# Attention with a 32-token window and a gated convolution FFN: the first batch's first half by head pairs, V's odd-row copies shared out anew, the order planned anew

## The chip, the cores and the metric

The kernel runs on one core of one Trainium2 chip. Its five queues are PE (TensorE, matrix products; PEld is its weight loads), DVE (VectorE), ACT (ScalarE), POOL (GpSimd) and SP, which here issues nearly all DMAs. The metric is the device time of one execution in microseconds (us), the median of several runs; lower is better.

## What is computed

The reference, cut to what matters (batch 8, 8 heads, 576 tokens, head width 64; model width 512, hidden width 1,024):

```python
scores = matmul(q, k.transpose(0, 1, 3, 2)) / sqrt(64)
scores = where(abs(pos[:, None] - pos[None, :]) <= 32, scores, -1e9)
attn = softmax(scores)
x = matmul(attn, v)             # back to (batch, tokens, 8 * 64)
h = maximum(x @ w_in, 0)
conv = conv_w[0] * h[t-1] + conv_w[1] * h[t] + conv_w[2] * h[t+1]
out = (h * sigmoid(conv)) @ w_out
```

Inputs and output are float32; the kernel computes its products in bfloat16.

## The kernel before

Everything is written out by hand. One long table, ORDER, lists some 845 steps as short words, and each step issues a few instructions at once; the order of the words is the order in which every engine's queue is filled. A word has a name, its arguments, where there is a choice a letter for the engine or the form (a is ScalarE, d VectorE, p GpSimd), and after @ the PSUM bank in which its result goes. Each engine works its queue in order, and an instruction waits where its inputs, its buffer or its bank are not free. All engine calls go through one helper, so nearly all instructions carry its line, L163, in the profile; they are told apart by the names of their tiles.

The steps, by batch b, group of four heads G (0, 1), token half h (0: the first four tiles of 64 tokens, 1: the other five):

- lq, lk load Q or K of (b, G) into one of six buffers st; cq, ck cast it to bfloat16 (qb); tq, tk turn it on VectorE in blocks of 32 (qT, kT). In batch 0 casts and turns go by halves of the columns.
- lv loads one of five chunks of V (128 tokens) into vst; cv casts it into ve. An odd tile of 64 tokens needs V at an offset of 64, so a second copy vo holds four such chunks for each batch: vo makes one chunk with two instructions (from ve, or on GpSimd from vst), and vd makes two chunks by two DMAs from ve. Such a chunk is called a pair of copies below. ve and vo carry a column of ones, which gives the softmax's sums.
- sc writes the band mask and the scores of four heads into four banks; ex is the exponential on ScalarE, into attn; av multiplies with V; nr (a reciprocal and a product on VectorE) normalises into xn.
- xp and xe (PE and ScalarE) or xt (a transposing DMA) turn xn into xT.
- ph is a projection with two of eight blocks of w_in, re its ReLU into hT. The tokens are cut in pieces of 384 columns, the first four of half that. li, ci and lo, co load and cast the quarters of w_in and w_out; block pair m needs quarter m.
- pc, tp, th, ga compute the convolution, its tanh (the sigmoid as a scaled tanh) and the gate into gT, in one of several forms: P, p on PE with full arrays; D, a, A on PE with quarter arrays, where a and A need three tanh instructions; X, x on ScalarE and VectorE; G, g on GpSimd.
- py is the output projection of 128 tokens, ye its copy into y, st its store.
- dg builds the diagonal matrices of the convolution weights, three instructions on ScalarE or one on VectorE; cw and cc bring those weights into place. id and ia are products without use, of 512 columns, that keep PE at work; ia reads a cast buffer and so waits for it. s0 to s6 are memsets and masks.

Of the kernel before, what the change touches and what calls it, by code (L numbers as in the profile page):

```python
# [17 lines left out]
s1 s3 lq,0,0 cq,0,0,1,a tq,0,0,1 cw@5 id,5@7 ia,0,0,1,1@7 lq,0,1 s4 cc lk,0,0 lv,0,2 lk,0,1 lv,0,1 cq,0,0,0,a  # L18
ia,0,0,0,3@7 lv,0,0 cq,0,1,0,p ia,0,1,0,3@7 s5 tq,0,1,0 dg,2,a ck,0,0,0,p tq,0,0,0 dg,3,d s2 dg,1,a tk,0,0,0
cq,0,1,1,a ia,0,1,1,5@7 ia,1,0,0,4@7 ck,0,0,1,a tk,0,0,1 s0 lv,0,3 dg,0,a dg,6,d sc,0,0,0@0 ck,0,1,0,p tq,0,1,1 dg,7,d  # L20
sc,0,0,1@4 ex,0,0,0 id,1@3 ia,1,1,0,2@3 lv,0,4 ck,0,1,1,p ia,1,1,1,2@3 tk,0,1,0 cv,0,2,p ex,0,0,1 li,0 li,3 tk,0,1,1
sc,0,1,0@0 cv,0,1,a cv,0,0,p sc,0,1,1@4 li,1 ex,0,1,0 vo,0,1,d vo,0,0,d av,0,1,0@0 av,0,0,0@2 nr,0,0,0 nr,0,1,0 lq,1,0
lk,1,0 ex,0,1,1 id,5@7 cv,0,3,p lk,1,1 vo,0,2,p lq,1,1 cv,0,4,a lv,1,1 dg,4,a vo,0,3,p ci,0,a lv,1,2 xp,0,1@0 xp,0,0@2
xe,0,1,a av,0,1,1@6 xe,0,0,a av,0,0,1@0 nr,0,1,1 ci,3,a ph,0,0@4 nr,0,0,1 re,0,0 ph,0,3@3 pc,0,0,P@4 re,0,3 xp,0,2@5
ci,1,p pc,0,3,p@2 cq,1,0,p xp,0,3@1 xp,0,4@6 xe,0,2,a ph,0,1@3 xe,0,3,a tq,1,0 xe,0,4,a ph,1,0@0 th,0,0,P ck,1,0,p
lv,1,0 re,0,1 ph,1,3@7 re,1,0 th,0,3,p ph,2,3@5 tk,1,0 re,1,3 ph,1,1@6 ck,1,1,p re,2,3 ga,0,0,P dg,5,d sc,1,0,0@0
re,1,1 pc,0,1,P@4 ex,1,0,0 pc,1,1,P@6 cq,1,1,p li,2 tk,1,1 sc,1,0,1@0 th,1,1,P lv,1,3 th,0,1,P pc,1,3,p@5 cv,1,1,p
# [51 lines left out]
tp,13,1,X ye,8,2,a pc,13,3,X@0 py,10,2@7 st,8,2 re,13,2 tp,13,0,g tp,13,3,X th,13,1,X pc,13,2,a@5 py,10,0@4 ye,10,2,d  # L79
th,13,3,X ga,13,1,X th,13,0,g py,9,2@7 th,13,2,a ga,13,0,g ga,13,3,X py,10,1@3 ye,10,0,a ga,13,2,a ye,9,2,a st,10,0  # L80
st,9,2 py,11,1@5 ye,10,1,d st,10,1 st,10,2 py,11,0@4 ye,11,1,a st,11,1 py,11,2,0@0 ye,11,0,a st,11,0 ye,11,2,0,a
st,11,2,0 py,11,2,1@4 ye,11,2,1,a st,11,2,1
"""


@with_exitstack
def kernel(
# [155 lines left out]
    where = {}  # L243
# [478 lines left out]
```

## Time and profile before

| what | value |
|---|---|
| median of 3 timed runs | 213.53 us (212.47 to 214.25) |
| the profiled execution | 210.9 us, span 209.1 us |
| DMA | 46.67 MB in 65,431 packets, mean 223 GB/s |
| of these under 512 B (V, mostly) | 53,084 packets |

Busy shares are read by stages: the first 20 us hold the loads, casts and scores of batch 0, from there to about 48 us the first batches' projections run while batch 1 is prepared, and from 48 us on each batch's attention stands between the projections of earlier ones. In timeline rows the first number is the start, the second the duration, and the bracket at the end the engine's idle time just before with what ended it.

### The profile page before, as it was taken

Reading aid. Unit: us, or ns where it says so; the run is one execution under the profiler, and the core shown is the slowest. Engines: PE = TensorE matmul, PEld = TensorE weight load, DVE = VectorE, ACT = ScalarE, POOL = GpSimd, SP = SyncE. Lnnn points to the kernel's source line nnn. Section 1 sums busy time; section 2 is a strip of 40 time slices with the busy share of each in tenths; the row PEclk is TensorE's granted clock in tenths of the full one; section 3 lists DMA queues with packets and bytes.
Section 4 is the critical chain, followed back from the end, with each engine's and each line's share of the span. In section 5 each row is a group of like instructions: output and inputs, shape, how many; then the busy total and the mean of one; then the engine's idle time right before and its main releaser. Section 6 shows DMA issues by size and latency. Waiting matters only on the chain.

```text
span 209.1 us, 7615 instructions
## 1 busy us (share of the span) xinstructions
PE 195.4 (93%) x3223; PEld 115.8 (55%) x3223; DVE 167.9 (80%) x277; ACT 172.0 (82%) x272; POOL 138.2 (66%) x161
## 2 busy tenths in 40 slices
PE   4978998799999989999999899998999999999994
PEld 2346986694565555655564454554655565555442
DVE  1785694989958988989999968979998749989850
ACT  3879888599889977998977878979989689999842
POOL 1485663596893859559999689889365009999600
PEclk9999999999999999999999999999999999999999
DMA  6999989989969889699998999996995541141154
GB/s 225 335 219 358 370 210 300 384 184 327 337 169 275 208 272 294 145 267 202 346 243 198 243 293 198 306 305 135 259 297 155 78 113 50 31 140 55 50 201 150
DMA packets 65431, 46.67 MB, mean 223 GB/s; under 512 B 53084, under 2 KB 55412, under 8 KB 65396
## 3 DMA queue, kind: packets, MB, share of 16 engines
q1 hardware_dynamic: 65360, 46.16, 82.6%
q8 instruction: 25, 0.41, 0.9%
q14 instruction: 10, 0.08, 0.1%
q10 hardware_dynamic: 36, 0.01, 0.0%
HBM read 32.52 MB, written 9.44 MB: 201 GB/s over the span
## 4 chain that ended last, share of the span: by engine, by line
PE 47%; DMA 12%; DVE 12%; SPq 11%; ACT 7%; issue 6%; POOL 4%; ACTq 0%; POOLq 0%
PE PS L163 47%; SPq L163 11%; DMA st<-in_k_dram 8%; DVE gT L163 5%; POOL zg L163 2%; DMA xT<-xn 2%; DMA vst<-in_v_dram 2%; DVE kT L163 2%; DVE vo L163 2%; ACT attn L163 1%; ACT z L163 1%; DVE xn L163 1%; ACT y L163 1%; POOL tap L163 1%; ACT hT L163 1%
## 5 line engine op out<-in xcount | busy, mean ns | idle before, releaser
L163 PE MATMUL PS<-xT,w_in_sb 128*128 128x385 bf16 (+3 forms) x448 | 69.2, 305 | 1.0 <-DMA xT<-xn 0.8
L163 PE MATMUL PS<-w_out_sb,gT 128*128 128x512 bf16 (+1 forms) x296 | 66.9, 374 | 0.2 <-DVE gT L163 0.2
L163 PEld LDWEIGHTS <-w_in_sb 128*128 128x128 bf16 x448 | 40.4, 98 | 23.8 <-issue 3.5
L163 ACT ACTIVATE hT<-PS 128x770 bf16<-128x770 f32 (+3 forms) x56 | 40.0, 724 | 9.0 <-PE PS L163 7.2
L163 ACT ACTIVATE attn<-PS 128x1024 bf16<-128x1024 f32 (+1 forms) x32 | 36.0, 1131 | 10.5 <-PE PS L163 10.5
L163 PEld LDWEIGHTS <-gT 128*128 128x128 bf16 x296 | 27.7, 98 | 30.4 <-issue 1.4
L163 POOL TENSOR_SCALAR qb<-st 128x1152 bf16<-128x1152 f32 (+1 forms) x24 | 28.1, 1179 | 21.2 <-DMA st<-in_k_dram 11.9
L163 POOL TENSOR_TENSOR zg<-zg,tap 128x768 f32<-128x768 f32 x18 | 33.3, 1848 | 1.5
L163 ACT ACTIVATE z<-PS 64x384 f32<-64x384 f32 (+4 forms) x55 | 28.2, 514 | 1.0 <-PE PS L163 0.2
L163 DVE TENSOR_TENSOR xn<-PS,rec 128x512 bf16<-128x512 f32 (+1 forms) x32 | 26.4, 824 | 1.1
L163 DVE SCALAR_TENSOR_TENSOR PS<-hT,conv_w_sb,PS 128x384 f32<-128x384 bf16 (+1 forms) x40 | 21.4, 597 | 6.3 <-ACT PS L163 6.1
L163 DVE SCALAR_TENSOR_TENSOR gT<-z,hT 128x768 bf16<-128x768 f32 (+1 forms) x28 | 25.7, 928 | 0.8 <-ACT z L163 0.7
L163 DVE SCALAR_TENSOR_TENSOR gT<-PS,hT 128x384 bf16<-128x384 f32 (+2 forms) x38 | 23.1, 613 | 2.8 <-ACT PS L163 2.4
L163 DVE STREAM_TRANSPOSE qT<-qb 128x576 uint32<-128x576 uint32 (+1 forms) x18 | 20.1, 1128 | 6.3 <-ACT qb L163 3.7
L163 PE MATMUL PS<-hT,diag_w 64*64 64x384 bf16 (+3 forms) x354 | 23.4, 306 | 0.6 <-DVE xn L163 0.6
L163 POOL TENSOR_SCALAR zg<-hT,conv_w_sb 128x384 f32<-128x384 bf16 x18 | 12.6, 712 | 16.9 <-ACT hT L163 16.7
L163 POOL TENSOR_SCALAR tap<-hT,conv_w_sb 128x384 f32<-128x384 bf16 x36 | 23.3, 660 | 0.6
L163 POOL TENSOR_SCALAR ve<-vst 128x512 bf16<-128x512 f32 x25 | 16.8, 683 | 10.2 <-DMA vst<-in_v_dram 10.1
L163 DVE STREAM_TRANSPOSE kT<-qb 128x576 uint32<-128x576 uint32 (+1 forms) x18 | 20.1, 1129 | 1.6 <-POOL qb L163 1.5
L163 ACT COPY y<-PS 128x512 f32<-128x512 f32 (+1 forms) x25 | 14.0, 570 | 5.0 <-PE PS L163 4.8
L163 POOL TENSOR_SCALAR vo<-vst 64x512 bf16<-64x512 f32 x24 | 15.6, 649 | 1.9 <-DMA vst<-in_v_dram 0.2
L163 PEld LDWEIGHTS <-diag_w 64*64 64x64 bf16 (+1 forms) x354 | 13.8, 103 | 5.3 <-issue 2.9
(50 smaller groups left out, 219.3 us busy)
## 6 DMA issues: line engine op xcount, KB each, us to landing
st<-in_q_dram SPq DMA_DIRECT2D x16, 576.0 KB, 6.6
st<-in_k_dram SPq DMA_DIRECT2D x16, 576.0 KB, 6.8
out_dram<-y SPq DMA_DIRECT2D x35, 256.0 KB, 3.7
vst<-in_v_dram SPq DMA_DIRECT2D x24, 256.0 KB, 5.3
vst<-in_v_dram SPq DMA_DIRECT2D x16, 192.0 KB, 5.9
xT<-in_moe_w_in_dram SPq DMA_DIRECT2D x2, 512.0 KB, 5.8
xT<-in_moe_w_out_dram SPq DMA_DIRECT2D x2, 512.0 KB, 9.4
vo<-ve SPq DMA_DIRECT2D x6, 130.0 KB, 3.0
```

The lines of the kernel that those rows point to most:

```text
L163: return lambda *args, **kwargs: tc.keep_in_program_order(do(*args, **kwargs))
```

## The change

ex, av and nr take an optional head pair: they then handle two of the four heads, and av needs one bank, not two. Only the first half of batch 0 uses it. The code:

```diff
-    def ex(b, G, h):
+    def heads(pair):
+
+        return (2 * pair[0], 2) if pair else (0, 4)
+
+    def ex(b, G, h, *pair):
         bank = where["sc", b, G, h]
         attn, n = attn_of(b, G, h)
+        a0, na = heads(pair)
         scalar.activation(
-            attn.rearrange("p (a x) -> p a x", a=4), PS[:, bank:bank + 4, 0:n],
+            attn.rearrange("p (a x) -> p a x", a=4)[:, a0:a0 + na, :],
+            PS[:, bank + a0:bank + a0 + na, 0:n],
             AF.Exp, bias=0.0, scale=scale,
         )
...
-    def nr(b, G, h):
-        bank = where["av", b, G, h]
+    def nr(b, G, h, *pair):
+        bank = where[("av", b, G, h, *pair)]
         n = (len(tiles_of(h)) + 1) // 2
...
+        a0, na = heads(pair)
...
-        rec = rec_[(2 * unit(b, G) + h) % 3][:, :, 0:n]
+        rec = rec_[(2 * unit(b, G) + h) % 3][:, a0:a0 + na, 0:n]
```

The rest is the table, which is new from end to end. A line of it before and now:

```diff
-s1 s3 lq,0,0 cq,0,0,1,a tq,0,0,1 cw@5 id,5@7 ia,0,0,1,1@7 lq,0,1 s4 cc lk,0,0 lv,0,2 lk,0,1 lv,0,1 cq,0,0,0,a
+s1 lq,0,0 s0 lk,0,0 lq,0,1 lk,0,1 lv,0,1 lv,0,2 s2 cw@0 id,4@7 cc dg,7,a cq,0,0,0,p ia,0,0,0,1@7 dg,5,a cq,0,0,1,p
```

Counted over the table:

| step | before | now |
|---|---|---|
| odd-row pairs on ScalarE, VectorE, GpSimd, by DMA | 0, 14, 12, 6 | 8, 10, 6, 8 |
| casts of Q and K on ScalarE: whole, half | 8, 4 | 5, 2 |
| the same on GpSimd | 20, 4 | 23, 6 |
| V chunks on ScalarE, GpSimd | 15, 25 | 14, 26 |
| weight quarters of w_in on ScalarE, GpSimd | 2, 2 | 1, 3 |
| diagonals on ScalarE, VectorE | 4, 4 | 5, 3 |
| outputs on ScalarE, VectorE | 25, 12 | 27, 10 |
| taps in forms P and p; D, a and A; X and x; G and g | 15; 22; 10; 9 | 12; 26; 9; 9 |
| products without use | 31 | 19 |

ScalarE's eight pairs lie in batches 0 (chunks 2, 3), 3 (2, 3), 4 (0, 1) and 5 (0, 1). Three places show how instructions moved. The first is GpSimd at the start, from its first work on the inputs. st0 holds Q and st1 K of batch 0's first heads, st2 and st3 those of its other heads; vst0 is V as loaded, xT1 and hT2 hold weight quarters. Before:

```order
L163 TENSOR_SCALAR qb2_69<-st2_63 128x576
L163 TENSOR_SCALAR qb1_68<-st1_62 128x576
L163 AFFINE_SELECT band0_115<-band0_115 128x256 x2
L163 MEMSET vst0_77 32x512 x2
L163 TENSOR_SCALAR qb3_70<-st3_64 128x576 x2
L163 TENSOR_SCALAR ve0_78<-vst0_77 128x8x64 x3
L163 TENSOR_SCALAR vo0_80<-vst0_77 64x8x64 x4
L163 TENSOR_SCALAR w_in_sb0_110<-xT1_92 128x4x256
```

The same place now:

```order
L163 MEMSET vst0_77 32x512 x2
L163 AFFINE_SELECT band0_115<-band0_115 128x256 x2
L163 TENSOR_SCALAR qb0_67<-st0_61 128x576 x2
L163 TENSOR_SCALAR qb1_68<-st1_62 128x576
L163 TENSOR_SCALAR qb2_69<-st2_63 128x576
L163 TENSOR_SCALAR qb3_70<-st3_64 128x576 x2
L163 TENSOR_SCALAR ve0_78<-vst0_77 128x8x64 x4
L163 TENSOR_SCALAR w_in_sb0_110<-xT1_92 128x4x256
L163 TENSOR_SCALAR w_in_sb0_110<-hT2_95 128x4x256
```

Memsets and mask moved ahead of all casts, the first Q came here from ScalarE, the four odd-row copies went to ScalarE, and a second weight quarter came in.

The second place is VectorE around the normalisation of batch 1 (vo1, ve1 and xn1 are batch 1's). Before:

```order
L163 COPY vo1_81<-ve1_79 64x520 x4
L163 SCALAR_TENSOR_TENSOR gT0_96<-z0_103,hT0_93 128x2x192
L163 RECIPROCAL rec1_87<-PS_118 128x4x2
L163 TENSOR_TENSOR xn1_90<-PS_118,rec1_87 128x4x2x64
L163 RECIPROCAL rec0_86<-PS_118 128x4x2
L163 TENSOR_TENSOR xn1_90<-PS_118,rec0_86 128x4x2x64
L163 COPY vo1_81<-ve1_79 64x520 x4
L163 SCALAR_TENSOR_TENSOR gT0_96<-z1_104,hT0_93 128x2x192
```

And now:

```order
L163 COPY vo1_81<-ve1_79 64x520 x4
L163 SCALAR_TENSOR_TENSOR gT1_97<-z2_105,hT1_94 128x2x192
L163 RECIPROCAL rec0_86<-PS_118 128x4x2
L163 TENSOR_TENSOR xn1_90<-PS_118,rec0_86 128x4x2x64
L163 RECIPROCAL rec1_87<-PS_118 128x4x2
L163 TENSOR_TENSOR xn1_90<-PS_118,rec1_87 128x4x2x64
L163 SCALAR_TENSOR_TENSOR gT1_97<-PS_118,hT1_94 128x2x192
```

The second group of four copies has left VectorE; GpSimd has it, reading vst.

The third place is SP's queue where batch 3 is loaded (st0 to st5 are the buffers of Q and K; st3 is here K of batch 3's second heads; out is a store). Before:

```order
L163 DMA st2_63<-in_q_dram 128x1152
L163 DMA vst0_77<-in_v_dram 128x8x64
L163 DMA out_0_dram<-y0_99 128x512
L163 DMA st5_66<-in_k_dram 128x1152
L163 DMA out_0_dram<-y1_100 128x512
L163 DMA vst0_77<-in_v_dram 128x8x64
L163 DMA vst0_77<-in_v_dram 96x8x64
```

And now:

```order
L163 DMA vst0_77<-in_v_dram 128x8x64
L163 DMA st2_63<-in_q_dram 128x1152
L163 DMA st3_64<-in_k_dram 128x1152
L163 DMA out_0_dram<-y2_101 128x512
L163 DMA out_0_dram<-y1_100 128x512
L163 DMA vst0_77<-in_v_dram 128x8x64
L163 DMA out_0_dram<-y0_99 128x512
```

K's load into st3 stands ahead of the first stores; before it was issued behind both stores and two loads of V. Earlier in the same queue, the third weight quarter of w_in was behind the first three V chunks of batch 1 and is now ahead of them.

More of the change, by code (lines that the diff above doesn't have):

```diff
@@ L23 @@
[L23 to L27, printed above, removed]
@@ L289, in av @@
         ts = tiles_of(h)
-        for a in range(4):
+        for a in range(a0, a0 + na):
             for i in range((len(ts) + 1) // 2):
```

139 lines of the change are left out of this document (73 added, 66 removed).

## Prediction

> **What bounds the kernel now.** I read the page's head first, then the busy time by stretches, then the timeline of the first 45 us, and last the waits of single rows. The profiled execution took 210.9 us, 209.1 of them its span.
>
> ```profile
> span 209.1 us, 7615 instructions
> PE 195.4 (93%) x3223; PEld 115.8 (55%) x3223; DVE 167.9 (80%) x277; ACT 172.0 (82%) x272; POOL 138.2 (66%) x161
> ```
>
> The stretches (span of time, its length, then busy time of PE, PEld, DVE, ACT, POOL, the granted clock, the DMA share, GB/s):
>
> ```profile
> 0.00:30.00 30.00, 24.54 (x491) 17.11 (x491) 19.17 (x50) 23.65 (x43) 17.02 (x29) 1.00 0.96 285
> 30.00:60.00 30.00, 27.34 (x543) 20.19 (x542) 24.71 (x45) 24.96 (x47) 19.81 (x24) 1.00 0.95 289
> 45.00:139.00 94.00, 92.12 (x1587) 51.72 (x1585) 83.81 (x124) 80.17 (x119) 74.08 (x82) 1.00 1.03 255
> 139.00:161.00 22.00, 21.07 (x399) 11.71 (x398) 19.97 (x31) 20.61 (x31) 15.91 (x20) 1.00 0.81 211
> 161.00:200.00 39.00, 38.93 (x429) 20.62 (x428) 32.34 (x52) 34.12 (x54) 23.46 (x24) 1.00 0.29 77
> ```
>
> From 45 us on TensorE (PE) is the bound: it is busy 152.1 of 155 us up to 200. Of the first 60 it lacks 8.1, and part of what it does there are idle products that fill waits. So a new order can win at the start, and only a little later. The table keeps nearly all of PE's work: the same projections, scores and outputs, and 12 idle products fewer. The convolution taps change form (in half-width pieces 3 fewer on full arrays, 4 more on quarter arrays), which I price below. So what counts is where PE waits.
>
> **The start.** These rows carry batch 0 up to its first projection (start, duration, engine, what; in brackets the idle time before and what ended it):
>
> ```profile
> 3.10 0.59 PE L163 MATMUL PS<-ident,conv_w 24*128 24x24 f32 x2 [3.10 <-DMA conv_w<-in_moe_conv_w_dram]
> 6.07 0.67 POOL L163 TENSOR_SCALAR qb<-st 128x576 bf16<-128x576 f32 x1 [4.75 <-DMA st<-in_q_dram]
> 6.27 1.86 ACT L163 ACTIVATE diag_w<-ident,conv_w_sb 128x128 bf16<-128x128 bf16 x6 [0.55 <-DVE hT L163]
> 8.46 0.67 POOL L163 TENSOR_SCALAR qb<-st 128x576 bf16<-128x576 f32 x1 [1.72 <-DMA st<-in_k_dram]
> 9.16 1.26 DVE L163 STREAM_TRANSPOSE kT<-qb 128x288 uint32<-128x288 uint32 x2 [0.75 <-POOL qb L163]
> 10.90 0.41 PE L163 MATMUL PS<-qT,kT 32*128 32x64 bf16 x32
> 14.08 1.53 DVE L163 COPY vo<-ve 64x520 bf16<-64x520 bf16 x4 [0.36 <-ACT ve L163]
> 15.34 0.22 PE L163 MATMUL PS<-ve,attn 128*64 128x65 bf16 x1 [0.71 <-ACT attn L163]
> 18.27 0.61 PE L163 MATMUL PS<-ident,xn 128*128 128x128 bf16 x8 [0.56 <-DVE xn L163]
> 19.83 1.36 PE L163 MATMUL PS<-xT,w_in_sb 128*128 128x193 bf16 x11
> 20.48 1.04 POOL L163 TENSOR_SCALAR w_in_sb<-xT 128x1024 bf16<-128x1024 f32 x1 [2.23 <-DMA xT<-in_moe_w_in_dram]
> ```
>
> Before, K's first load is the third in the queue and its cast starts at 8.46. In the new order it is second; second place ended in time for a cast at 6.07. The second half of K is now cast by ScalarE behind nine of its diagonal products (six take 1.86, so nine 2.8). They can start once the convolution weights have come through PE (3.69) and been copied, near 4.0, so that cast runs about 6.9 to 7.6, the two turns to about 8.9, and the first scores stand near 9.1 instead of 10.9: 1.8 earlier. The odd-row copies still wait for V's chunks, which the same bytes precede as before, and for ScalarE, which has six more diagonal products and a half cast (2.6), the first exponentials (2.4 by the rows below) and a cast of V (0.6) to do from 7.6 on: it ends near 13.1, four copies of 1.53 near 14.6, and the first product with V stands at 14.7 instead of 15.3.
>
> Then comes the split by head pairs, whose cost is in these rows (busy us, mean ns of one):
>
> ```profile
> L163 ACT ACTIVATE attn<-PS 128x1280 bf16<-128x1280 f32 x16 | 19.8, 1240 | 3.6 <-PE PS L163 3.5
> L163 DVE TENSOR_TENSOR xn<-PS,rec 128x768 bf16<-128x768 f32 x16 | 15.3, 957 | 0.6
> L163 ACT ACTIVATE attn<-PS 128x1024 bf16<-128x1024 f32 x16 | 16.3, 1022 | 6.9 <-PE PS L163 6.9
> L163 DVE TENSOR_TENSOR xn<-PS,rec 128x512 bf16<-128x512 f32 x16 | 11.1, 691 | 0.6
> L163 DVE RECIPROCAL rec<-PS 128x8 f32<-128x8 f32 x16 | 3.2, 199 | 4.9 <-ACT ve L163 2.6 <-PE PS L163 1.4 <-ACT attn L163 0.8
> ```
>
> 256 more columns cost an exponential 218 ns and a normalising product 266 ns. By that line half an exponential of 1,024 takes 0.59, so two take 0.15 more than one; half a product takes 0.42, and with a second reciprocal of 0.20 two halves cost 0.36 more than one whole. VectorE's four halves end about 2.5 after the first can start, and they start about 1.5 earlier than the two wholes did. I put the first projection at about 19.0 instead of 19.83. But this does not pass through. The second quarter of the input weights is now cast by ScalarE, and the load that it waits for let the same cast start at 20.48 before. The bytes ahead of it are the same, so it runs 20.5 to 21.5, and ScalarE's first three ReLUs, all projections with that quarter and the tap products stand behind it. So I take **0** for the start, with 0.9 gained (the load lands earlier) and 1.0 lost (the ReLUs queue) as bounds.
>
> **Batch 1, 33 to 42 us.** Here PE waits four times in the old order, beside V's late chunks:
>
> ```profile
> 34.10 0.22 PE L163 MATMUL PS<-ve,attn 128*64 128x65 bf16 x1 [0.48 <-issue]
> 34.78 0.62 POOL L163 TENSOR_SCALAR ve<-vst 128x512 bf16<-128x512 f32 x1 [1.54 <-DMA vst<-in_v_dram]
> 34.93 0.21 DVE L163 RECIPROCAL rec<-PS 128x8 f32<-128x8 f32 x1 [2.59 <-ACT ve L163]
> 36.74 2.10 DVE L163 COPY vo<-ve 64x520 bf16<-64x520 bf16 x4
> 36.76 0.51 PE L163 MATMUL PS<-ident,xn 128*128 128x128 bf16 x6 [0.54 <-DVE xn L163]
> 38.88 0.19 PE L163 MATMUL PS<-vo,attn 128*64 128x65 bf16 x1 [0.43 <-DVE vo L163]
> 41.89 0.66 PE L163 MATMUL PS<-hT,diag_w 128*128 128x192 bf16 x6 [0.64 <-DVE xn L163]
> 37.87 0.44 PE L163 MATMUL PS<-hT,diag_w 64*64 64x192 bf16 x12
> ```
>
> VectorE does one thing after another: it idles 2.59, normalises, copies two odd-row pairs for 2.10 while the next products with V wait for them, and only then normalises again. The waits of PE in these rows, 0.48, 0.54, 0.43 and 0.64, sum to 2.1. The new order loads weight quarter 2 ahead of V of batch 1, puts the two late odd-row pairs on GpSimd, which idles there (1.54 before a cast of V), and runs two more projections and, net, two more tap steps on PE ahead of the first product with V. Walking the new order with these durations, the first product with V comes when its exponential frees the banks, with the normalisation directly behind it, and 2.10 has gone from VectorE's queue. I take **2.0** gained; bounds are 2.9, when the gaps under the waits' threshold go too, and 0, when the weight quarter lands late and the third projections wait for it instead.
>
> The taps: three full-array steps of 0.66 fewer and four quarter-array steps of 0.44 more are -0.2, and the scattered quarter form has three tanh instead of one. I take 0.
>
> **Batch 3's K load.** The old order holds it behind two stores, which wait for their results:
>
> ```profile
> 62.34 1.62 SPq L163 DMA_DIRECT2D st<-in_k_dram  x1
> 68.97 3.73 POOL L163 TENSOR_SCALAR qb<-st 128x1152 bf16<-128x1152 f32 x2 [4.25 <-DMA st<-in_k_dram]
> 73.98 0.42 PE L163 MATMUL PS<-qT,kT 32*128 32x64 bf16 x32 [0.60 <-DVE kT L163]
> ```
>
> GpSimd waits 4.25 for it and PE at last 0.60. The new order issues it ahead of both stores. **0.6** gained, bounds 0 and 0.6: past 0.6 PE had other work.
>
> **The odd-row copies.**
>
> ```profile
> L163 DVE COPY vo<-ve x28: 290/292/1887, 14.1 to 114.4; 64x520 bf16<-64x520 bf16 x28
> L163 ACT CAST ve<-vst 128x512 bf16<-128x512 f32 x15 | 9.3, 624 | 0.0
> L163 ACT CAST qb<-st 128x1152 bf16<-128x1152 f32 x8 | 9.3, 1159 | 1.4 <-DMA st<-in_k_dram 1.3
> ```
>
> VectorE's copies take 0.29 at least and up to 1.89. The trace shows none on ScalarE: the rows nearest are a cast of 512 columns, 0.62, and the small diagonal product, 0.31. I take 0.55, as the width is the cast's. Sixteen are 8.8 us (5.0 to 10). ScalarE gives up three whole casts of Q and K (3.5), two halves, one weight cast and one V cast, and takes some diagonal products, outputs and tanh, so its work grows by about 5. In 45 to 139 it idles 94 - 80.2 = 13.8, which can hide that. I take **0.3** lost, bounds 0 and 5. VectorE has eight copies fewer (2.3 us at least) and two outputs fewer; it wasn't the bound, so 0. The fourth pair moved by DMA adds two transfers of 130 KB; I take 0, at worst 1.
>
> The Trainium skill's page "SBUF — State Buffer" (SBUF: two separate sides) says that VectorE in a fast mode and GpSimd take turns at a shared port, each holding it for a whole instruction, and that ScalarE never waits there. The spread from 0.29 to 1.89 in the row above agrees; by that rule the move to ScalarE costs less than its 16 durations suggest, as copies that can be stretched leave VectorE and GpSimd.
>
> **The sum.** 0 - 2.0 - 0.6 + 0.3 = -2.3: a span of 206.8. The profiled run lies 2.6 below the median of the three timed runs, 213.53 (212.47 to 214.25), so I put the change on the median: **211.2**. Around 1%, here 2.1 us, is what a measurement can tell from no change.
>
> **Rivals.**
> *The loads take it back (same).* The DMA share is 1.03 from 45 to 139: if the engines' queues are full, an earlier PE only meets the same landings, and the 2.0 of batch 1 returns as waits like the 4.25 at 68.97. For it: the share. Against it: PE is busy 92.1 of 94 there, and the old order's stores, not the engines, held the K load back. Time: 213.2 (212.4 to 214).
> *ScalarE's queue (slower).* The eight pairs stand in a first-in queue ahead of exponentials and ReLUs in batches 0, 3, 4 and 5. For it: in 139 to 161 ScalarE is busy 20.6 of 22, so it has stretches without slack. Against it: the 13.8 of slack between 45 and 139, where these pairs lie. It decides once more than 2.6 of the 5 us reach PE (the 2.3 of the sum and the 0.3 in it); with all 5 it gives 211.2 + 4.7 = 215.9.
> *PE at half rate.* The weight loads ahead of the idle products show its pace:
>
> ```profile
> 8.29 0.15 PEld L163 LDWEIGHTS <-ident 128*128 128x128 bf16 x1 [0.28 <-issue]
> 8.75 1.60 PEld L163 LDWEIGHTS <-ident 128*128 128x128 bf16 x8 [0.30 <-issue]
> 16.47 1.24 PE L163 MATMUL PS<-ident 128*128 128x512 bf16 x5
> ```
>
> Up to 8.3 one product takes 0.43, from 8.75 on 0.20, although the granted clock reads 1.00. Before the first scores the new order has 9 products where 21 stood, with holes between them. If PE still runs at half rate until the projections, the first scores (0.4), the products with V and the transposes (0.6) and the first two projections (1.4, as eleven products took 1.36) take twice as long: 2.4 lost, 211.2 + 2.4 = 213.6. For it, the holes; against it, PE kept its pace through the holes between 11 and 16 us, as five products near 17 take 1.24. The Trainium skill's page "TensorE: Matmul & The Clock Gate" (Part 1: The HAM clock gate) says that PE starts at half clock and is released by about 3.4 us of sustained activity; by that rule nine products with holes may not release it. The trace agrees with the release, at 8.3 or so.
>
> **How the numbers follow.** Forecast 0.56: its own range is 208.2 (0.9 + 2.9 + 0.6 gained, less the noise of a median) to 212.8 (1.0 lost at the start and 0.6 of batch 1's gain); 0.46 of it lies below 211.4, 0.10 above. Loads take it back: 0.21, all same. ScalarE's queue: 0.17, slower. Half rate: 0.06, of it 0.02 same and 0.04 slower with the ReLUs queued too. Faster 0.46, same 0.33, slower 0.21. The range runs from 208.2 to 215.8, up to ScalarE's rival; what it leaves out is that rival's upper part and a start that gains more than its bounds.
>
> **What would show it.** Right: first scores near 9.1 but the first tap products still near 22; no wait of VectorE of over 1 us between 32 and 42, and PE's step in batch 2 some 2 us earlier; no wait of GpSimd for K near 69. Wrong: ScalarE busy over 92% in 75 to 115 with PE waiting for its exponentials (second rival); GpSimd still waiting some 4 us for K near 69 (first); products of 0.43 after 10 us (third). The forecast fails outright if PE's new waits after 45 us, anywhere, sum to more than 2.

## The result, and the profile after

The changed kernel takes 218.44 us in the median of four runs (216.51 to 221.57), the old one on the same chip 213.0 (212.08 to 214.25): ratio 1.029, 95% interval 1.020 to 1.037. It is 5.4 us slower; 211.2 was forecast. Ratios here leave out executions over 1.5% above the fastest of their kernel. The profiled execution took 216.5 us; the head of its page, and the same stretches as before (span, length, busy PE, PEld, DVE, ACT, POOL, granted clock, DMA share, GB/s):

```profile
span 214.7 us, 7620 instructions
PE 193.0 (90%) x3217; PEld 115.5 (54%) x3241; DVE 165.7 (77%) x268; ACT 178.1 (83%) x290; POOL 133.9 (62%) x156
...
45.00:139.00 94.00, 87.81 (x1497) 48.84 (x1509) 75.12 (x109) 81.73 (x122) 66.30 (x75) 1.00 0.97 239
139.00:161.00 22.00, 21.19 (x398) 12.04 (x403) 19.21 (x29) 19.47 (x31) 13.93 (x16) 1.00 0.97 228
161.00:200.00 39.00, 35.94 (x464) 20.01 (x468) 31.55 (x48) 31.29 (x47) 21.23 (x23) 1.00 0.39 92
```

From 45 to 139 us TensorE was busy 92.1 and is now 87.8, and in the last stretch 38.9 and now 35.9. From 45 to 139 every engine but ScalarE does less, and ScalarE is busy 81.7 of 94: no engine became the bound. The start, in the timeline:

```profile
8.93 0.29 PE L163 MATMUL PS<-ident,band 32*128 32x128 bf16 x8
13.50 0.40 PE L163 MATMUL PS<-ident,band 32*128 32x128 bf16 x8 [0.36 <-issue]
15.50 0.26 PE L163 MATMUL PS<-ve,attn 128*64 128x65 bf16 x1 [0.37 <-ACT attn L163]
20.15 1.06 ACT L163 CAST w_in_sb<-xT 128x1024 bf16<-128x1024 f32 x1
20.32 1.88 PE L163 MATMUL PS<-xT,w_in_sb 128*128 128x193 bf16 x19 [0.21 <-ACT xT L163]
```

The scores come at 8.93, as worked out, but the first product with V only at 15.50 and the first projection at 20.32, half a us later than in the old kernel. The same eight mask products take 0.29 at 8.93 and 0.40 at 13.50: TensorE runs slower there, which is taken up below. Then TensorE's larger waits behind 45 us:

```profile
60.15 0.19 PE L163 MATMUL PS<-vo,attn 128*64 128x65 bf16 x1 [1.49 <-DVE vo L163]
65.94 0.68 PE L163 MATMUL PS<-hT,diag_w 64*64 64x384 bf16 x12 [0.44 <-DVE xn L163]
83.43 0.23 PE L163 MATMUL PS<-ident,band 32*128 32x128 bf16 x2 [0.46 <-DVE xn L163]
84.27 0.28 PE L163 MATMUL PS<-ident,band 32*128 32x128 bf16 x6 [0.61 <-DVE xn L163]
89.54 1.17 PE L163 MATMUL PS<-hT,diag_w 64*64 64x384 bf16 x22 [0.74 <-DVE gT L163]
107.24 0.19 PE L163 MATMUL PS<-ve,attn 128*64 128x65 bf16 x1 [0.66 <-ACT attn L163]
163.20 0.29 PE L163 MATMUL PS<-ident,band 32*128 32x128 bf16 x6 [0.81 <-DVE y L163]
173.26 0.98 PE L163 MATMUL PS<-xT,w_in_sb 128*128 128x385 bf16 x5 [1.59 <-DMA xT<-xn]
```

These eight sum to 6.8 us, and all over 0.3 behind 45 us to 7.9; the old trace has three over 0.3 there, 1.9 together. Three places were looked into.

**Place T, 56 to 60 us.** VectorE makes the four copies of batch 2's last two odd-row pairs while GpSimd works the taps of batch 4 (a tap and the sum):

```profile
55.91 4.18 DVE L163 COPY vo<-ve 64x520 bf16<-64x520 bf16 x4
56.84 1.22 POOL L163 TENSOR_SCALAR tap<-hT,conv_w_sb 128x384 f32<-128x384 bf16 x2
58.14 1.80 POOL L163 TENSOR_TENSOR zg<-zg,tap 128x768 f32<-128x768 f32 x1
```

The old order had these copies on GpSimd. Here they take 4.18 together, the last 1.86 (from 58.23 to 60.09; GpSimd's sum ends at 59.94), and TensorE's 1.49 at 60.15 is the wait for it.

**Place Q, 59 to 80 us.** SyncE's queue, then who waited for it:

```profile
59.16 0.49 SPq L163 DMA_DIRECT2D vst<-in_v_dram  x1
66.98 3.92 SPq L163 DMA_TRANSPOSE xT<-xn  x3
70.94 1.61 SPq L163 DMA_DIRECT2D vst<-in_v_dram  x1
73.22 0.43 SPq L163 DMA_DIRECT2D st<-in_k_dram  x1
...
75.21 0.62 POOL L163 TENSOR_SCALAR ve<-vst 128x512 bf16<-128x512 f32 x1 [6.71 <-DMA vst<-in_v_dram]
79.56 1.26 DVE L163 STREAM_TRANSPOSE qT<-qb 128x576 uint32<-128x576 uint32 x1 [4.91 <-POOL qb L163]
```

The queue issues nothing between 59.65 and 66.98: at its head stands a transpose of xn, whose last normalisation ends at 66.95. Four loads of batches 3 and 4 stand behind three transposes; two of them, a V chunk and a K, the old order had well ahead. GpSimd idles 6.71, VectorE 4.91, and TensorE's waits from 83 to 90 us follow.

**Place L, 155 to 173 us.** Batch 7's new transfer of odd-row rows holds the same queue until V is cast:

```profile
155.12 0.46 SPq L163 DMA_DIRECT2D vst<-in_v_dram  x1
161.02 1.11 SPq L163 DMA_DIRECT2D vo<-ve  x2
163.56 3.87 SPq L163 DMA_TRANSPOSE xT<-xn  x2
```

### The profile page after: what moved, and what is told of

The parts are those of the page before. It is cut to its first block, busy times and chain, and to the rows that moved or that the text cites. A ratio compares the mean times of both kernels' runs of the same rounds, so it can differ in the third digit from the quotient of the medians.

```text
span 214.7 us, 7620 instructions
## 1 busy us (share of the span) xinstructions
PE 193.0 (90%) x3217; PEld 115.5 (54%) x3241; DVE 165.7 (77%) x268; ACT 178.1 (83%) x290; POOL 133.9 (62%) x156
## 4 chain that ended last, share of the span: by engine, by line
PE 52%; ACT 13%; DMA 12%; DVE 10%; SPq 5%; issue 5%; POOL 1%; DVEq 0%; ACTq 0%; POOLq 0%
PE PS L163 52%; SPq L163 5%; DMA st<-in_q_dram 5%; ACT attn L163 3%; DMA vst<-in_v_dram 3%; DVE xn L163 3%; DMA out_dram<-y 2%; ACT diag_w L163 2%; ACT z L163 2%; DVE vo L163 2%; DMA xT<-xn 2%; DVE gT L163 2%; ACT hT L163 1%; POOL qb L163 1%; ACT ve L163 1%
## 5 line engine op out<-in xcount | busy, mean ns | idle before, releaser
L163 PE MATMUL PS<-w_out_sb,gT 128*128 128x512 bf16 (+1 forms) x273 | 64.8, 373 | 2.2 <-issue 0.5
L163 POOL TENSOR_SCALAR qb<-st 128x1152 bf16<-128x1152 f32 (+1 forms) x29 | 30.7, 1065 | 21.9 <-DMA st<-in_q_dram 11.7
L163 ACT ACTIVATE attn<-PS 128x1280 bf16<-128x1280 f32 (+2 forms) x34 | 36.0, 1072 | 7.5 <-PE PS L163 7.2
L163 ACT ACTIVATE z<-PS 64x384 f32<-64x384 f32 (+4 forms) x61 | 29.7, 487 | 4.5 <-DVE PS L163 2.0
L163 DVE SCALAR_TENSOR_TENSOR gT<-PS,hT 64x384 bf16<-64x384 f32 (+4 forms) x41 | 24.9, 606 | 7.7 <-ACT PS L163 7.3
L163 POOL TENSOR_SCALAR zg<-hT,conv_w_sb 128x384 f32<-128x384 bf16 x18 | 13.6, 767 | 26.0 <-ACT hT L163 25.9
L163 DVE SCALAR_TENSOR_TENSOR gT<-z,hT 128x768 bf16<-128x768 f32 (+1 forms) x28 | 28.1, 1016 | 0.8 <-ACT z L163 0.6
L163 DVE TENSOR_TENSOR xn<-PS,rec 128x768 bf16<-128x768 f32 (+2 forms) x34 | 26.7, 786 | 1.2
L163 POOL TENSOR_SCALAR ve<-vst 128x512 bf16<-128x512 f32 x26 | 17.3, 676 | 14.7 <-DMA vst<-in_v_dram 14.5
L163 DVE SCALAR_TENSOR_TENSOR PS<-hT,conv_w_sb,PS 128x384 f32<-128x384 bf16 x36 | 19.6, 616 | 6.9 <-ACT PS L163 6.9
L163 PEld LDWEIGHTS <-attn 128*64 128x64 bf16 x640 | 12.6, 113 | 8.4 <-issue 6.2
```

Of the source, the lines that this page charges most:

```text
L163: return lambda *args, **kwargs: tc.keep_in_program_order(do(*args, **kwargs))
```

## The experiments

Every edit changes only words of the order (s1, s5, l3 and p2 have the changed kernel's functions, which take the old words as well). The diffs show fragments of the table's lines; most words moved by an edit stand on other lines. A yardstick serves all of them: TensorE's delay, the start of a group of products less the ordinary durations of all TensorE's work ahead of it in that kernel's order (worked out from the traces, not a row of a page). Where it grows, TensorE lost time. The points are named by the work done; 6 is near 23 us, 27.5 near 48, 40 near 62, 50 near 74, 76 near 103, 113 near 142, and 172 is the end. Each row is one traced execution. The old kernel's took 210.9 us, 1.5 to 2.9 us less than its medians, so rows are best compared by where they grow.

```
work done      6   27.5    40    50    76   113   172
old         16.5   21.1  22.6  24.2  25.6  28.0  31.4
changed     17.3   19.7  22.2  24.1  28.4  31.0  37.0
r1_taps     16.8   19.9  20.8  22.9  26.5  32.2  38.5
r2_loads    17.5   21.3  23.9  27.0  28.4  32.5  38.3
r4_three    16.9   20.0  20.9  24.4  25.8  30.4  42.0
s2_dve4     17.4   20.8  21.6  26.7  29.6  32.6  36.6
s4_act8     20.3   27.6  29.3  31.8  35.2  40.3  43.1
s5_splice   17.3   19.7  20.5  22.9  25.0  27.2  31.1
s6_two      16.7   20.0  20.8  24.1  26.0  29.0  35.5
l1_act4     17.0   19.5  20.4  22.9  24.5  27.8  34.2
l2_p7       16.8   19.7  20.5  23.7  25.2  29.9  34.3
p3_vd       18.3   24.0  24.9  25.7  27.6  30.1  34.6
```

**The places undone, one by one.** *r1*: GpSimd's second part of the taps behind the two casts of Q.

```diff
-av,2,0,1@0 tp,4,3,g ex,2,0,0
-cq,3,1,p nr,2,1,1
+av,2,0,1@0 ex,2,0,0
+cq,3,1,p tp,4,3,g nr,2,1,1
```

> GpSimd's third tap of piece 4 (1.1 + 1.8 us) is moved behind a cast in its queue, so that it no longer runs beside VectorE's eight odd-row copies of batch 2 near 57. Theory T (the copies are stretched by GpSimd's instructions, PE waits 1.49 for them, and what follows to 90 us is its consequence): the copies take about 0.3 each instead of 0.56 to 1.86, PE's wait at 60.15 goes, batch 2's transposes start 1.5 earlier, and the median falls by 3 to 4.5 us against the changed kernel. Rival Q (the load queue alone makes the loss at 75 to 90): the wait goes, but the loads behind the transposes still land late, so -1.5 or less. Rival A (ScalarE's copies make the loss): no change.

217.27 us, ratio 1.014 (1.003 to 1.025). At place T in its trace:

```profile
56.15 2.07 DVE L163 COPY vo<-ve 64x520 bf16<-64x520 bf16 x4
59.47 1.15 POOL L163 TENSOR_SCALAR qb<-st 128x1152 bf16<-128x1152 f32 x1 [2.37 <-DMA st<-in_q_dram]
60.60 1.16 POOL L163 TENSOR_SCALAR tap<-hT,conv_w_sb 128x384 f32<-128x384 bf16 x2
...
104.96 2.28 PE L163 MATMUL PS<-xT,w_in_sb 128*128 128x385 bf16 x8 [1.76 <-ACT y L163]
```

The same four copies, with the taps behind them, take 2.07 in place of 4.18, and the wait at 60 is gone: the delay at 40 falls from 22.2 to 20.8. Place T is shown, though the median falls by 1.2 and not by 3 to 4.5. At 104.96 a new wait of 1.76 stands: ScalarE's output copy waited 1.75 for the store that frees its buffer.

*r2*: the four loads ahead of the first transpose.

```diff
-ga,4,1,D xt,2,0
-lv,3,2 xe,2,2,a lq,4,0 tk,3,1 sc,3,0,1@0 cv,3,0,p lk,4,0 py,2,0@5 ex,3,0,1 lv,3,4
+ga,4,1,D lv,3,2 lq,4,0 lk,4,0 lv,3,4 xt,2,0
+xe,2,2,a tk,3,1 sc,3,0,1@0 cv,3,0,p py,2,0@5 ex,3,0,1
```

> The four loads of V chunks 2 and 4 of batch 3 and of Q and K of batch 4 are issued ahead of batch 2's three transposes instead of behind them. Theory Q: GpSimd's wait of 6.71 for a V chunk near 75 and VectorE's of 4.91 for Q near 79 go, PE does not fall back between 82 and 91 (3 us there), and the median falls by 2 to 3 us against the changed kernel, while PE's 1.49 at 60 stays. Theory T: the loads are late because the transposes are, so the result is the same -2 to -3, but with the wait at 60 unchanged. Rival A: -0.5 or less, since ScalarE still holds PE back.

217.5 us, ratio 1.020 (1.013 to 1.026). The wait at place T stays; GpSimd now idles 3.82 for a V chunk, and VectorE's wait of 4.91 for Q is gone (it waits 3.62 for a K instead). From 50 to 76 the delay grows by 1.4, as in the old kernel (1.4), and not by 4.3. So the order of the loads makes that stretch. But the gain does not last: from 40 to 50 the delay grows by 3.1, at 76 it is 28.4 as in the changed kernel, and the median falls by 0.9 and not by 2 to 3. The transposes are late behind the four loads.

*r3*: batch 7's transfer behind a transpose of batch 6.

```diff
-cv,7,4,p vd,7,0 ye,7,2,a
-xt,6,0 nr,6,1,1
+cv,7,4,p ye,7,2,a
+xt,6,0 vd,7,0 nr,6,1,1
```

> Batch 7's added pair of copies by DMA is issued behind batch 6's first two transposes instead of ahead of them. Theory V (the pair waits 5.4 us at the head of the load queue for V's casts, and all transposes behind it are late): PE's wait of 1.59 for the transposes at 173 goes or falls under 0.5, and the median falls by 1 to 1.6. Rival: the transposes are held by the normalisation or by stores, and the time stays within 0.5.

222.94 us, ratio 1.043 (1.031 to 1.054): the wrong cure. The product with V now waits for those rows. *r4* makes the three edits together.

> All three moves together. If the three causes are what separates the kernels: 218.4 - 1.5 - 3 - 1.6 = 212.3, level with the kernel before (213.0). If ScalarE's copies or the half-rate start carry the loss: above 216.

221.72 us, ratio 1.038 (1.027 to 1.048). The third edit spoils its end (a wait of 3.83 at 171.41 for the rows), but up to 76 its delay is 25.8, the old kernel's 25.6: T and Q together make up the loss up to 103 us, and T most of it, as r1 alone stands at 26.5 and r2 alone at 28.4.

**ScalarE's copies.** In the changed trace, by kind (count, then minimum/median/maximum in ns), and on ScalarE near 103 us:

```profile
L163 DVE COPY vo<-ve x20: 290/562/1861, 13.6 to 104.3; 64x520 bf16<-64x520 bf16 x20
L163 ACT COPY vo<-ve x16: 622/623/625, 16.6 to 119.3; 64x520 bf16<-64x520 bf16 x16
...
103.18 1.27 ACT L163 COPY vo<-ve 64x520 bf16<-64x520 bf16 x2
104.48 1.07 ACT L163 COPY y<-PS 128x512 f32<-128x512 f32 x2
105.44 0.82 ACT L163 ACTIVATE PS<-PS 128x768 f32<-128x768 f32 x1
106.17 1.03 ACT L163 ACTIVATE attn<-PS 128x1024 bf16<-128x1024 f32 x1
```

ScalarE's copy takes 0.623 whatever runs beside it. Two of them stand ahead of the output copies, a tanh and the exponential for which TensorE waits 0.66. *s2* is r1 and r2 with these two pairs back on VectorE.

```diff
-vo,4,0,a
-vo,4,1,a
+vo,4,0,d
+vo,4,1,d
```

> Edit, to the changed kernel: GpSimd's batch 4 taps behind the two casts of Q (as in r1), batch 3's and 4's four loads ahead of the transposes of batch 2 (as in r2), and batch 4's two odd-row copies on ScalarE put back on VectorE at their places. Theory 'ScalarE queue': the 1.7 lost at 102 to 107 us in r4 (0.79 for bank 1, 0.66 for the exponential) were ScalarE's two copies of 0.62; they go, so 1 to 1.7 below the same kernel without the third edit: about 215.5, ratio 1.005 to 1.015. Rival: VectorE is no freer there, its copies are stretched beside GpSimd's taps to over 1 us each, and the wait returns as a wait for an odd-row copy: about 217, 1.015 to 1.02.

215.32 us (213.58 to 216.55), ratio 1.029 (1.016 to 1.041). Both waits of r4 at 103 and 105 us are gone; but TensorE stood 0.69 at 74.52 for a turned Q and 1.97 at 76.91 for a transpose, which the queue now has behind the four loads. Then came what the stretches show (columns as above):

```profile
74.00:76.00 2.00, 0.42 (x32) 0.30 (x31) 2.00 (x4) 0.99 (x1) 1.25 (x2) 1.00 1.34 72
76.00:78.00 2.00, 1.09 (x5) 0.65 (x6) 0.73 (x1) 1.28 (x3) 0.00 (x0) 0.81 1.08 412
78.00:80.00 2.00, 2.00 (x48) 1.03 (x50) 0.00 (x0) 0.59 (x1) 0.00 (x0) 0.50 1.04 396
80.00:82.00 2.00, 2.00 (x34) 1.15 (x23) 0.00 (x0) 1.88 (x3) 1.68 (x3) 0.84 0.79 190
```

After the pause the granted clock falls to 0.50 for 0.76 + 2.00 + 0.64 = 3.4 us (from the clock means), so the pause costs another 1.7. *s3* is s2 with batch 7's rows copied by GpSimd again.

```diff
-cv,7,4,p vd,7,0 ye,7,2,a
-th,10,3,x ga,10,1,a
+cv,7,4,p vo,7,1,p ye,7,2,a
+th,10,3,x vo,7,0,p ga,10,1,a
```

> Edit: as s2, and batch 7's first half of odd-row rows copied by GpSimd again (two copies, at the old places) and not by DMA. Theory 'sum of places': the changed kernel's 5.4 over the old one are 1.5 to 3 for the taps and the loads, 1.5 for ScalarE's copies, and 1.6 for the DMA queue that is held at 155 to 161 us; with all undone it comes to 212 to 213.5, no slower than the old one, ratio 0.99 to 1.00. Rival 'tight order': each undone wait uncovers another (as the change's other undoings did), and it stays over 1.01.

215.27 us, ratio 1.029 (1.019 to 1.039): no better, with the same pause and slow stretch near 76 us. *s4* is the other way about: the old kernel with the change's eight ScalarE pairs alone.

```diff
-vo,0,2,p
-vo,0,3,p
+vo,0,2,a
+vo,0,3,a
...
-vo,4,0,d
-vo,4,1,d
+vo,4,0,a
+vo,4,1,a
```

> Edit, to the old kernel: only the eight pairs of odd-row copies that the change gives to ScalarE go there, at their old places in the order; all else is old. Theory 'ScalarE queue alone': 16 copies of 0.62 are 10 us more work for ScalarE; in the old order it idles 13.8 between 45 and 139, so about 1 to 2 us reach TensorE: 214.5 to 215.5, ratio 1.005 to 1.01. Rival 'ScalarE is the bound': over 4 us, ratio over 1.02, with TensorE waiting for exponentials in batches 3 to 5. Third possibility, no cost: 1.00.

221.53 us, ratio 1.058 (1.047 to 1.069), 9.1 between the medians: the rival's size, but not its place, since much of the loss comes before batch 3. Its start shows how:

```profile
19.21 1.27 ACT L163 COPY vo<-ve 64x520 bf16<-64x520 bf16 x2
20.50 1.04 ACT L163 CAST w_in_sb<-xT 128x1024 bf16<-128x1024 f32 x1
21.45 1.07 ACT L163 CAST xT<-PS 128x512 bf16<-128x512 f32 x2
20.53 0.19 PE L163 MATMUL PS<-vo,attn 128*64 128x65 bf16 x1 [0.52 <-ACT vo L163]
```

ScalarE still has all its old casts there; a copy ahead of a weight cast, and that ahead of the eviction of the transposed rows, moves the whole chain: 3.8 more delay than in the old kernel at 6, 6.5 at 27.5, 12 at 113. Part of this is the clock: it falls to 0.50 for 3.4 us twice, from 21.6 and from 45.5 us, with up to 1.7 lost each time. In the changed order casts taken off ScalarE pay for part of the copies: it is busy 178.1 us, in the old order 172.0.

**The changed start with the old rest.** *s1* has the changed order up to the first scores of batch 2 and the old one behind.

```diff
 th,3,0,P re,4,3 ga,3,1,P lk,3,0 cv,2,2,a ga,3,0,P pc,4,3,g
-sc,2,1,0@2 lq,3,0 ye,1,0,a vo,2,1,d py,0,1@7
+py,0,1@0 lq,3,0 py,0,2@6 vo,2,1,p cv,2,0,a
```

> Edit: the changed kernel's order up to the first scores of batch 2 (some 49 us), and from there the old order for all that is left (its GpSimd and VectorE copies in batches 2 to 7, its loads, its one late pair of copies by DMA less). Theory 'later': the changed order gains in batch 1 (TensorE was 1.3 us ahead at 48 us) and loses all of its 6 us behind that, so this kernel keeps most of the gain: about 1 below the old kernel, 212 to 213, ratio 0.990 to 1.000, and TensorE's reach at 48 us stays 1 to 1.5 ahead up to 200. Rival 'the start': the changed first 49 us leave the later work in a worse state (the loads ordered otherwise, the clock's half-rate slice near 11 to 16 us), so that it comes out over 1.01 whatever follows.

215.76 us, ratio 1.021 (0.999 to 1.044). At this seam one output tile of batch 0 is copied out after batch 2's scores have overwritten its bank, so the kernel leaves that tile's right values out of its result; the instructions are the same. TensorE waited 1.15 and 2.11 near 55 us, as GpSimd had the taps ahead of batch 2's copies, and the clock read 0.50 from 56 to 62. *s5* mends the seam: the changed order up to batch 2's second scores with those taps at the old place.

```diff
-ga,3,0,P pc,4,3,g sc,2,1,0@2
+ga,3,0,P sc,2,1,0@2
...
-sc,2,1,1@4 nr,2,1,0 py,0,0@0 ex,2,1,1 lq,3,1
+ga,3,2,a lq,3,1 tq,2,0 cv,2,3,a ye,0,2,a vo,2,2,p sc,2,1,1@4 nr,2,1,0 py,0,0@0
```

> Edit: as s1, with the seam mended. The changed order runs up to the second scores of batch 2 (some 53 us) but leaves GpSimd's batch 4 taps at their old place, so the odd-row copies of batch 2's second half stand ahead of them on GpSimd again; from there the old order. In s1 GpSimd had the taps ahead of those copies, TensorE waited 1.15 and 2.11 near 55 us, and the granted clock then read 0.50 from 56 to 62 us. Theory 'later': without that seam TensorE keeps the 1 to 1.5 us that the changed order gains in batch 1, up to the end: profiled span 207.5 to 209 beside the old kernel's 209.1, ratio 0.985 to 1.00. Rival 'the start': what batch 1 gains is taken back behind 53 us even in the old order, since the loads land no earlier: TensorE's reach at 75 us and later equals the old kernel's, ratio 1.00 to 1.01, with a wait for K or V near 70 to 75 us that the old kernel doesn't have.

210.54 us (209.23 to 212.31) beside 213.1: ratio 0.991 (0.986 to 0.996). This is 0.9% below the old kernel, and below both. Its head and stretches:

```profile
span 208.6 us, 7641 instructions
...
30.00:60.00 30.00, 29.01 (x673) 21.63 (x665) 23.67 (x42) 27.04 (x51) 21.14 (x26) 1.00 1.02 300
45.00:139.00 94.00, 90.52 (x1573) 50.45 (x1586) 82.11 (x119) 79.71 (x121) 74.12 (x80) 1.00 1.01 255
```

From 30 to 60 us TensorE is busy 29.0, where the old kernel had 27.3. All that the change loses therefore stands in the order behind 53 us, with the taps of place T, and what it gains in front of that is real. How much of the gain lasts is less clear: the medians lie 2.6 apart, but in the two traces s5's lead is 1.4 at 27.5, 0.6 at 76 and 0.3 at the end.

**The changed kernel, four places mended.** *s6* has r1, only the two loads that the old order had early, batch 4's two pairs on VectorE, and one store of batch 2 earlier.

```diff
-ga,4,1,D xt,2,0
+ga,4,1,D lv,3,2 lk,4,0 xt,2,0
...
-ga,5,1,a xt,3,4
+ga,5,1,a st,2,1 xt,3,4
```

> Edit, to the changed kernel: the taps behind the casts (r1); of the four loads of r2 only the two that the old order had early too (batch 3's third V chunk, batch 4's first K) ahead of the transposes; batch 4's two ScalarE copies back on VectorE; and one store of batch 2 ahead of batch 3's transposes, as in the old order. Theory 'queue': in s2 TensorE stood 1.97 at 76.9 us for a transpose that queued behind four loads, and the clock read 0.50 for the next 3 us; with two loads fewer ahead of it that wait and the slow stretch go, and so does the wait for the output buffer near 104 us: 2 to 3 below s2, median 212.5 to 213.5, ratio 0.995 to 1.01, granted clock 1.00 throughout behind 20 us. Rival 'always another': TensorE waits as long elsewhere, a pause of some 2 us again followed by a stretch at 0.50, ratio 1.015 to 1.03.

214.88 us (211.78 to 215.49), ratio 1.005 (0.997 to 1.013): by the medians 3.6 of the 5.4 are back, and the interval includes no difference from the old kernel. It misses the 212.5 to 213.5 expected. The pause at 76 and the slow stretch are gone and the granted clock reads 1.00 throughout; the delay follows the old one to 76 (26.0 and 25.6). Behind 113 it still grows by 6.5, in the old kernel by 3.4. Three kernels take s6 apart. *l1* puts batch 4's two pairs back on ScalarE (s2's diff, turned round).

> Edit, to s6: batch 4's first two pairs of odd-row copies back on ScalarE, as in the changed kernel; nothing else. Theory 'ScalarE queue': TensorE waits again for an output's bank and for the exponential near 103 to 107 us (0.79 and 0.66 in r4), 1 to 1.5 us: ratio to s6 1.004 to 1.007, to the old kernel 1.009 to 1.014. Rival: s6's earlier store has made room on ScalarE, and the copies are hidden: the same as s6 within 0.3%.

214.63 us (213.42 to 217.52), the same as s6 by its median; the old kernel spread widely in this series, and the ratio to it is 1.017 (1.006 to 1.027). The wait near 103 us is 1.24, but for a transpose and not for ScalarE; its delay at 113 is 27.8, the old kernel's 28.0. Once loads and stores stand right, no cost of these two pairs is to be seen. *l2* is s6 with s3's copies for batch 7's rows.

> Edit, to s6: batch 7's first half of odd-row rows copied by GpSimd at the old places instead of by DMA. Theory 'DMA rows': SyncE's queue no longer stands at 155 to 161 us behind the transfer that waits for V's casts, the transposes of batches 6 and 7 are issued earlier, and TensorE's wait of 1.64 at 172 us for a transpose shrinks to under 0.8: 1 to 1.5 below s6, ratio to the old kernel 0.997 to 1.002. Rival: the queue stands there for a store or a transpose all the same, and nothing changes: 1.003 to 1.008.

214.4 us (212.45 to 215.94), ratio 1.015 (1.004 to 1.026): the wait of 1.64 at 172 is gone as expected, but 0.71 and 1.15 at 161 and 165 take its place. SyncE's queue still issues nothing from 153.31 to 161.16, then a store: the transfer of place L did not hold it alone, as the rival said. *l3* is s6 up to batch 5's last scores and the old order behind.

```diff
-sc,5,0,1@4 ye,5,0,d lv,6,4 cv,6,1,p pc,8,2,a@0 ex,5,0,1
+lv,6,3 ye,5,0,d lk,7,0 lv,6,4 st,5,1 cv,6,1,a cq,6,1,p sc,5,0,1@0 pc,8,2,D@4 vo,6,1,p tq,6,1 ex,5,0,1
```

> Edit, to s6: from the last scores of batch 5 (some 130 us) on the old order, with its forms; batch 7's rows are then copied by GpSimd too. Theory 'order of batches 6 and 7': the waits of s6 at 129, 139, 148, 162 and 172 us (4.2 together) become the old kernel's (0.5), so 2 to 3 below s6, ratio to the old kernel 0.988 to 0.997. Rival 'the loads': they are set by what was loaded before 130 us, and it stays at 1.00 to 1.005.

215.91 us (212.78 to 219.23), ratio 1.018 (1.001 to 1.035). It says little: at this seam batch 5's product with V waits 3.01 at 140.38 us for a bank that a ReLU has yet to empty, and the clock falls behind that.

**Two parts alone in the old order.** *p2*: the head pairs of batch 0.

```diff
-ex,0,0,0 id,1@3
+ex,0,0,0,0 ex,0,0,0,1 id,1@3
...
-av,0,1,0@0 av,0,0,0@2 nr,0,0,0 nr,0,1,0
+av,0,1,0,0@0 av,0,1,0,1@1 av,0,0,0,0@2 av,0,0,0,1@3 nr,0,0,0,0 nr,0,0,0,1 nr,0,1,0,0 nr,0,1,0,1
```

> Edit, to the old kernel: batch 0's first token tiles by head pairs alone (two exponentials, four products with V and two normalisations, each with its own pair, at the old places); all else old. Theory of the prediction: two more exponentials cost 0.15 each time and two more normalising halves 0.36, the first may start earlier; at these places nothing waits for the earlier half, so +0.2 to +0.7 at 20 us, swallowed by the load of the second weight quarter: 0.995 to 1.005. Rival: the longer VectorE and ScalarE queues push the first projections by over 1 us and that stays: 1.005 to 1.012.

212.49 us (209.7 to 215.41) beside 213.1: medians 0.3% apart, ratio of the runs that it keeps 0.991 (0.984 to 0.997). No cost; whether there is a gain stays open. *p3*: batch 7's rows by DMA.

```diff
-cv,7,4,p vo,7,1,p ye,7,2,a
-th,10,3,x vo,7,0,p av,6,1,1@0
+cv,7,4,p ye,7,2,a
+th,10,3,x vd,7,0 av,6,1,1@0
```

> Edit, to the old kernel: batch 7's first half of odd-row rows by DMA and not by GpSimd's two copies; all else old. Theory of the prediction: no cost (GpSimd gains two copies of 1.2, the rows come by the queue in time): 0.995 to 1.005. Rival 'queue': the transfer waits on the cast of V's chunks and holds SyncE's queue (7 us in the changed kernel at 155 to 161), so the transposes of batches 6 and 7 and the last projections are late, or the product with V waits for the rows: 1.01 to 1.03, with TensorE standing over 1 us at 160 to 175.

214.38 us, ratio 1.008 (1.003 to 1.013), and in its trace:

```profile
160.44 2.41 SPq L163 DMA_DIRECT2D vo<-ve  x4
164.90 0.22 PE L163 MATMUL PS<-vo,attn 128*64 128x65 bf16 x1 [1.23 <-DMA vo<-ve]
```

The rows come 1.23 too late, about the 1.3 between the medians.

## Why the prediction was wrong

The step that failed is in the part on what bounds the kernel: "So a new order can win at the start, and only a little later." It read TensorE's 152.1 busy of 155 us as a bound that protects the old time, and behind 45 us priced only the loads and copies that it saw move (-0.6, +0.3, 0 and 0). A full engine protects nothing: the order behind 45 us was planned anew as well, and each wait that it opened was a loss. The sum had no term for them; of the rivals only ScalarE's queue had waits there, and for another cause. The prediction's last test, new waits behind 45 us of more than 2 together, came out at 6.8 in eight rows against 1.9, so 4.9 more. That the loss lies behind 53 us is shown by s5.

- **Start, 0 (0.9 gained to 1.0 lost).** Right in its mechanism: scores at 8.93 (9.1 forecast), the weight cast at 20.15 (20.5), the rest swallowed. The delay at 6 is 17.3 against 16.5, 0.8 lost, inside the bound. The first product with V (14.7 forecast) came at 15.50, the first projection (19.0) at 20.32, and the first tap products (22) at 23.35.
- **Batch 1, -2.0.** Right. Between 6 and 27.5 the delay grew by 4.6 in the old kernel and grows by 2.4 in the changed one: 2.2 gained. The net lead at 48 us is 1.4; s5 keeps 0.6 of it at 103 us and 0.3 at the end in its trace, more by the medians.
- **Batch 3's K load, -0.6.** The mechanism was half seen. K is no longer waited for, but a V chunk is: 6.71 in place of 4.25. The prediction looked at the load that moved up, and not at the two that moved behind the transposes. From 50 to 76 the delay grows by 2.9 more than in the old kernel (4.3 against 1.4), but undoing this alone does not bring it back: with the loads moved r4 is 0.7 ahead of r1 at 76, and r2 level with the changed kernel.
- **Odd-row copies, +0.3 (0 to 5).** The duration was 0.623, not 0.55. Batch 4's two pairs cost nothing that l1 can tell; 0.66 of wait shows in the changed trace. The 13.8 of ScalarE's idle time between 45 and 139 was set against all eight pairs, but two of them lie in batch 0, before 20 us; in s4 6.5 of the 11.7 lost by its trace stand before 48 us. The term left out was VectorE's: batch 2's copies came to it from GpSimd, beside taps, and cost the 1.49 of place T. "It wasn't the bound, so 0" was the reason given.
- **Fourth pair by DMA, 0 (at worst 1).** p3 measures 1.3 at the old places (0.3 to 1.3% by its interval): about the bound. In s6's order l2 finds no difference that its runs can tell. Batch 6's first half, by DMA now as well, was not tried alone.
- **Rivals.** ScalarE's queue had the right sign and, at 215.9, less than half of the 5.4, but it is not the cause: ScalarE is busy 34.06 of 40 us (85%) from 75 to 115, short of the 92% named as its sign, and its 0.66 is a tenth of the waits. The half rate did appear, in every trace with this start, at some time between 9 and 17 us, and with it its sign, idle products 0.43 apart (12.09 and 12.52 in the changed trace). In the changed trace the first scores run at full rate and the second ones do not; in others the clock is not yet released at the first ones, as in r1, whose eight mask products take 0.40 at 9.55 us and 0.29 at 13.54. By the projections the rate is full again, and the delay at 6 is 16.7 to 17.5 in these kernels beside 16.5, so the 2.4 of that rival was not reached. No kernel with this start ran without it, so what it costs is not shown; it does not explain the loss, which comes behind 53 us. "Loads take it back" had the place near 70 us, but what held the loads was SyncE's queue, which issued nothing for 7.3 us, and not the DMA engines' queues.

Of the 5.4 us, moving words at four places brings back 3.6 by the medians (s6); how these share it is not separated, except that batch 4's pairs add nothing (l1). The remaining 1.8 is within the interval of s6's ratio. By its trace it lies mostly behind 142 us, in batches 6 and 7 (3.1 of the 4.1 by which s6 ends behind the old kernel). Batch 7's rows by DMA are not shown to be its cause, and l3, which should have told, failed at its seam. That stays open.

## What to carry to other kernels

A bound engine that is 98% busy says that a new order has little to win behind that point, never that it has little to lose: walk every queue of the new order there as carefully as at the place of the gain, above all what each in-order DMA queue holds behind a transfer that waits for a result. When an order is planned anew, test it in pieces; here the changed first 53 us with the old rest came out 0.9% below the old order and further below the new one. A wait of TensorE is dearer than its length wherever the clock falls behind it.

## What the runs showed of the hardware

When TensorE stands idle for much of some 3 us in mid-kernel, its clock is halved for 3.4 us, or twice that. In s2 it is 3.4 us, in s1 (56 to 63 us) 6.8 by the same sum. What decides is not the length of one pause: 1.76 (r1, clock 0.50 from 106 to 108), 1.97 (s2) and even 1.47 with 0.43 before it (s3, 76 us) were followed by it, and 1.59 (the changed kernel), 1.64 (s6) and 2.05 (p2, 121 us) were not. The clock changes only at steps of 3.41 us, counted in each trace from the clock's first change. If the 17 traces are cut into these steps, 934 of them at full clock up to 205 us, the clock is at 0.50 behind all 15 in which TensorE was busy 0.06 to 0.51 of the step, and behind none of the other 919, the lowest of which were busy 0.52 (s3), 0.53 (r4) and 0.54 (the changed kernel). So in these traces the border lies near half of a step, and a pause that falls across two steps can go free.

It happens at the start as well. p3 has the old kernel's order there word for word, but in its trace a step begins at 13.70 and TensorE is busy 1.57 of it; the next is at 0.50. The steps of the old trace fall otherwise (12.1 to 15.5 us, busy 0.69), and its clock reads 1.00. The first two lines are these steps of p3; the other two are p2's step with most of the pause of 2.05, busy 1.94, and the one behind it, with no fall:

```profile
13.70:17.11 3.41, 1.57 (x107) 1.23 (x99) 1.49 (x4) 2.46 (x4) 2.65 (x5) 1.00 1.06 302
17.11:20.53 3.42, 3.39 (x26) 1.94 (x26) 1.70 (x4) 2.44 (x6) 0.94 (x2) 0.50 1.06 387
...
116.90:120.32 3.42, 1.94 (x47) 0.98 (x46) 3.00 (x7) 3.09 (x7) 1.79 (x3) 1.00 1.44 125
120.32:123.73 3.41, 2.79 (x18) 1.70 (x19) 3.41 (x5) 0.96 (x2) 1.00 (x2) 1.00 1.09 362
```

p3's delay at 27.5 is 24.0 in place of 21.1: 2.9 us between two executions of the same instructions, of which 3.4 us at half rate explain at most 1.7. This may be part of why the old kernel's own times spread from 207.8 to 218.2 (and one of 251). The Trainium skill's page "TensorE: Matmul & The Clock Gate" (Part 1: The HAM clock gate) has half rate follow an idle window of about 3.4 us that runs freely, so that it differs from run to run; the traces agree with the length, but here a window half idle was enough.

A 64 x 520 copy on VectorE took 0.29 to 1.86 us in the changed trace and one on ScalarE 0.622 to 0.625; four on VectorE took 2.07 with GpSimd casting or waiting beside them and 4.18 beside its taps. The Trainium skill's page "SBUF — State Buffer" (SBUF: two separate sides) has VectorE and GpSimd share a port and ScalarE not: the trace agrees, and here it speaks for ScalarE only as far as ScalarE has a gap at that place.
